# Down projection of a GeGLU feed-forward block: all 28 F blocks by Strassen, with a 20-block ring for the right operands

## The chip, the cores and the metric

The kernel runs on one core of one Trainium2 chip. The metric is the device time of one execution in microseconds; lower is better.

## The reference

```python
def setup_inputs():
    B, S, D, F = 1, 2048, 1024, 3584
    # x [B,S,D], w_gate [D,F], w_up [D,F], w_down [F,D]: bfloat16, normal * 0.05

def reference(x, w_gate, w_up, w_down):
    return (gelu_tanh(x @ w_gate) * (x @ w_up)) @ w_down
```

F is 28 blocks of 128. The kernel takes x in two halves of 1024 rows, and each half in two groups of 512 rows. For each half it makes the hidden tensor `hT` (gate, gelu, up, product), then two down groups.

## The kernel before

Nearly all matmuls are part of Strassen's scheme: a 2x2 product of blocks with seven block products M1 to M7 in place of eight. Sums of left operands are S1 to S4, of right operands T1 to T4. M1 and M2 read the bf16 tensors themselves; the other five read sums, or copies, held in fp32r (a 32-bit float type). B11 to B22 are the four quarters of a right operand, A11 to A22 those of a left one. A gate/up "pair" of F blocks takes 16 bf16 and 40 fp32r matmuls. A down group works on 11 block columns of each half of F by Strassen and on the 6 blocks left over by plain bf16 matmuls:

```python
NS = 11                                    # Strassen blocks in each half of K
NKK = (KF - 2 * NS) // WDT                 # 3 tiles of 2 plain blocks
t_mem = ...[P, max(5 * KH * TB, 2 * NS * DN)]   # right operands, two sets of 11
...
def down_group(hT, h, grp, then):          # then: work issued behind a product
    product("m1", PB, h_block(0, 0), wd_block(0, 0), True)
    product("m5", VB, lsum(0), rsum(0), True, behind=two(to_s2_t2))
    load_wd_to(base + 3)
    product("m2", PB, h_block(0, 1), wd_block(1, 0))
    product("m6", QB, lsum(0), rsum(0), behind=two(to_s4_t4), order=tail)
    product("m7", RB, lsum(1), rsum(1), behind=lambda i: t_down("b22", i, i + 1), order=head)
    ...                                    # additions; plain matmuls of bank set PB
    product("m3", QB, lsum(0), rsum(1), behind=two(next_s1_t3) if more else None)
    product("m4", RB, lsum(1), rsum(0), behind=two(next_t1) if more else None)
    ...                                    # the other plain matmuls, evacuation, stores
```

T2 and T4 of w_down are made once, while the pairs of the first half run ("staging": three subtractions for each block, the results stored to DRAM), and reloaded in each group by the SP queue (the queue in which SyncE issues transfers one after the other). In the first half the same queue also brings in the x of the second half, by transposing DMAs of one slice of 128 x 512 each, and the gate and up weights of its first pairs.

Two other places matter. In the startup, plain units (gate and up of one F block by bf16 matmuls, gelu, product) run while the operands of the first pair are made; in the passage to the second half, those of its first pair are made behind the down group:

```python
# startup                                  # passage, behind products of group 1
unit(hT, (0, 0), 0, 1)                     then1["m3"] = [lambda: w_fill(0)]
for name in S_NAMES:                       then1["m4"] = [t_sum t1, t2, t3]
    for j in range(2):                     then1["plain"] = [
        s_sum(0, PPG, j, name)  # GpSimd       t_sum b22, s_fill,  # s_fill: GpSimd
t_sum("t4")                     # GpSimd       t_sum t4,           # GpSimd
for fi in range(1, FPG):                       lambda: w_fill(1),
    unit(hT, (0, 0), fi, 1)                ]
```

## Time and profile before

| | before |
|---|---|
| time, median of 3 runs | 548.70 us (548.59 to 548.71) |
| span of the profiled run | 546.8 us |
| first matmul of the first down group | 187.13 us |
| first matmul of the second half | 277.07 us |
| first matmul of its first down group | 453.46 us |
| TensorE's gap at the end of the startup, from one matmul's start to the next | 0.36 us, from 36.45 us |

The page of the profile, the chain and the startup are shown and read in the prediction below.

### The profile page before, as it was taken

The page shows a single profiled execution, that of the slowest core. Times are in us where ns is not written, and L with a number is a line of the kernel's source. Part 1 is how long each engine was busy: PE and PEld are TensorE (multiplying, and loading weights), DVE is VectorE, ACT ScalarE, POOL GpSimd, SP SyncE. Part 2 cuts the span into 40 slices and gives each one's busy share as a digit, 9 for nine tenths or more (in the row PEclk, how much of TensorE's full clock was granted, in tenths as well). Part 3 has the DMA queues.
Part 4 walks back from the last instruction along what each step waited for, and adds up shares of the span by engine and source line. Part 5 has one row for each costly group of instructions (what it writes and reads, how often), then busy time and mean ns, then how long its engine had stood idle before and what let it go on. Part 6 is the DMA issues. An engine that isn't in the chain of part 4 may idle for free.

```text
span 546.8 us, 7160 instructions
## 1 busy us (share of the span) xinstructions
PE 538.7 (99%) x2390; PEld 364.9 (67%) x2433; DVE 305.4 (56%) x416; ACT 252.8 (46%) x446; POOL 253.4 (46%) x216
## 2 busy tenths in 40 slices
PE   8999999999999999999999999999999999999997
PEld 3456677777677667557667766777667776775673
DVE  1716666665566998934534444444444469986412
ACT  2435555555555317225365555555555542333161
POOL 0487767777666000000499776677776720000000
PEclk9999999999999999999999999999999999999999
DMA  9743364563725799579932240404040419904922
GB/s 271 229 133 122 98 226 142 166 196 113 230 79 192 254 345 292 144 264 319 331 130 78 76 130 24 155 1 154 0 155 5 150 61 316 352 4 161 354 102 77
DMA packets 69700, 90.65 MB, mean 166 GB/s; under 512 B 15904, under 2 KB 46624, under 8 KB 69664
## 3 DMA queue, kind: packets, MB, share of 16 engines
q1 hardware_dynamic: 69120, 89.67, 50.4%
q10 hardware_dynamic: 544, 0.52, 0.3%
q8 instruction: 20, 0.33, 0.2%
q14 instruction: 16, 0.13, 0.1%
HBM read 77.07 MB, written 9.96 MB: 159 GB/s over the span
## 4 chain that ended last, share of the span: by engine, by line
PE 97%; DMA 1%; issue 1%; ACT 0%; ACTq 0%
PE bank L368 60%; PE bank L569 33%; PE bank L232 5%; DMA w_mem<-in_w_up_dram 1%; PE bank L290 0%; ACT o_sb L721 0%; ACTq L155 0%
## 5 line engine op out<-in xcount | busy, mean ns | idle before, releaser
L368 PE MATMUL bank<-t_mem,s_mem 128*128 128x512 f32 x1040 | 255.2, 400 | 0.0
L368 PEld LDWEIGHTS bank<-t_mem,s_mem 128*128 128x128 f32 x1040 | 195.5, 188 | 45.2
L342 POOL TENSOR_TENSOR s_mem<-w_mem 128x512 fp32r<-128x512 bf16 x104 | 125.7, 1229 | 187.1 <-DMA w_mem<-in_w_gate_dram 112.0
L391 DVE TENSOR_TENSOR bank<-bank,m 128x512 f32<-128x512 f32 x104 | 72.4, 699 | 98.8 <-ACT bank L411 89.7
L251 DVE TENSOR_TENSOR hT<-w_mem,bank 128x512 bf16<-128x512 f32 x112 | 76.6, 687 | 63.9 <-ACT w_mem L246 31.1
L246 ACT ACTIVATE w_mem<-bank 128x512 f32<-128x512 f32 x112 | 66.4, 597 | 87.5 <-DVE bank L391 52.7
L569 PE MATMUL bank<-t_mem,s_mem 128*128 128x512 f32 x440 | 104.4, 395 | 0.0
L368 PE MATMUL bank<-xT,w_mem 128*128 128x512 bf16 x391 | 95.2, 380 | 1.5
L569 PEld LDWEIGHTS bank<-t_mem,s_mem 128*128 128x128 f32 x440 | 82.6, 188 | 18.4
L368 PEld LDWEIGHTS <-w_mem 128*128 128x128 bf16 x416 | 36.7, 98 | 50.5 <-issue 13.3
L569 PEld LDWEIGHTS <-hT 128*128 128x128 bf16 x368 | 34.9, 98 | 43.8 <-issue 3.7
L342 POOL TENSOR_TENSOR s_mem<-s_mem,w_mem 128x512 fp32r<-128x512 f32 x52 | 61.2, 1198 | 0.0
L342 POOL TENSOR_TENSOR s_mem<-w_mem,s_mem 128x512 fp32r<-128x512 bf16 x52 | 60.0, 1175 | 0.0
L499 DVE TENSOR_TENSOR t_mem<-w_mem 128x1024 fp32r<-128x1024 bf16 (+2 forms) x54 | 52.5, 1020 | 0.0
L355 ACT CAST s_mem<-w_mem 128x512 fp32r<-128x512 bf16 x52 | 31.9, 615 | 32.5 <-PE bank L368 29.1
L569 PE MATMUL bank<-wd_sb,hT 128*128 128x512 bf16 x184 | 41.4, 379 | 0.5
L569 PE MATMUL bank<-w_mem,hT 128*128 128x512 bf16 x169 | 39.0, 380 | 0.4
L406 ACT COPY m<-bank 128x512 f32<-128x512 f32 x52 | 30.5, 587 | 17.6 <-PE bank L368 17.6
L411 ACT COPY bank<-bank 128x512 f32<-128x512 f32 x52 | 29.6, 570 | 17.1 <-PE bank L368 17.1
L402 ACT COPY bank<-bank 128x512 f32<-128x512 f32 x52 | 29.6, 570 | 13.7 <-PE bank L368 13.7
L721 ACT CAST o_sb<-bank 128x512 bf16<-128x512 f32 x28 | 14.4, 620 | 43.9 <-PE bank L569 43.9
L548 DVE TENSOR_TENSOR s_mem<-hT 128x512 fp32r<-128x512 bf16 (+3 forms) x36 | 27.8, 804 | 6.6 <-PE bank L368 3.4
(31 smaller groups left out, 195.9 us busy)
## 6 DMA issues: line engine op xcount, KB each, us to landing
t_mem<-t_dram SPq DMA_DIRECT2D x32, 512.0 KB, 5.1
w_mem<-in_w_gate_dram SPq DMA_DIRECT2D x11, 1024.0 KB, 5.5
w_mem<-in_w_up_dram SPq DMA_DIRECT2D x11, 1024.0 KB, 7.9
w_mem<-in_w_down_dram SPq DMA_DIRECT2D x8, 1024.0 KB, 7.5
t_mem<-t_dram SPq DMA_DIRECT2D x24, 256.0 KB, 5.9
wd_sb<-in_w_down_dram SPq DMA_DIRECT2D x12, 512.0 KB, 5.7
wd_sb<-in_w_down_dram SPq DMA_DIRECT2D x22, 256.0 KB, 7.2
t_dram<-o_sb SPq DMA_DIRECT2D x22, 256.0 KB, 2.1
```

What stands on the lines that cost most here:

```text
L246: act(nc.scalar.activation(out=g_sb, in_=ps[:], func=ACT.Gelu_apprx_tanh))
L251: nc.vector.tensor_tensor(out=hT[:, fc, tb * TB : (tb + 1) * TB], in0=g_sb, in1=ps[:], op=ALU.mult,)
L342: pool(nc.gpsimd.tensor_tensor(out=t, in0=in0, in1=in1, op=op))
L355: act(nc.scalar.copy(out=t, in_=a(1, 1)))
L368: nc.tensor.matmul(banks[bank][:], lhsT=lhs[:, c, :], rhs=rhs[:, c, :], start=start and c == 0, stop=c == KH - 1, skip_group_check=True,)
L391: nc.vector.tensor_tensor(out=banks[dst][:], in0=banks[src][:], in1=m5[j][:], op=ALU.add)
L402: act(nc.scalar.copy(out=banks[QB[j]][:], in_=banks[PB[j]][:]))
L406: act(nc.scalar.copy(out=m5[j][:], in_=banks[VB[j]][:]))
L411: act(nc.scalar.copy(out=banks[RB[j]][:], in_=banks[QB[j]][:]))
L499: dve(nc.vector.tensor_tensor(out=t, in0=in0, in1=in1, op=ALU.subtract))
L548: dve(nc.vector.tensor_tensor(out=t, in0=in0, in1=in1, op=op))
L569: nc.tensor.matmul(banks[bank][:], lhsT=lhs, rhs=rhs, start=start, stop=stop, skip_group_check=True,)
```

## The change

The intent is to give the six plain blocks to Strassen too, which takes 196 matmuls for a group in place of 202. The operands of 14 blocks no longer fit in two fixed sets, so five right operands (T1, T2, T3, B22, T4) follow one another through a ring of 20 blocks, each new block in the place of one that has been read; B21 of w_down is streamed in as an operand of M2, and M2 moves behind M7. Staging covers 14 blocks, of which three move into the startup. T4 of gate/up, and the S sums of the second half's first pair, move from GpSimd to VectorE.

```diff
-    NS = 11
-    NKK = (KF - 2 * NS) // WDT
+    NS = KF // 2
+    NR = 20
-    t_mem = shared_pool.tile([P, max(5 * KH * TB, 2 * NS * DN)], F32R, name="t_mem")
+    t_mem = shared_pool.tile([P, NR * DN], F32R, name="t_mem")
@@ t_sum
             t2 = tsum["t2"].bitcast(F32)
-            pool(nc.gpsimd.tensor_tensor(out=t, in0=b(1, 0), in1=t2, op=sub))
+            dve(tt(out=t, in0=b(1, 0), in1=t2, op=sub))
@@ the ring
+    SEQ = ("t1", "t2", "t3", "b22", "t4")
+    def right(grp, name, i0, i1):
+        r0 = ((grp * len(SEQ) + SEQ.index(name)) * NS + i0) % NR
+        t = t_mem[:, r0 * DN : (r0 + i1 - i0) * DN]
@@ down_group, after M5 (B21 is loaded here, T2 to T4 behind the product before)
+        for q in range(4):
+            load_b21(n, q)
+        done("m5")
+        product("m6", QB, lsum(0), rsum("t2"), False, False, behind_m6, tail)
+        ...
+        def behind_m7(i):
+            if NT2 + i < NS:                       # NT2 = NR - NS = 6
+                t_down(grp, "b22", NT2 + i, NT2 + i + 2)
+            else:
+                t_down(grp, "t4", NT2 + i - NS, NT2 + i - NS + 2)
+        product("m7", RB, lsum(1), rsum("t3"), False, False, behind_m7, head)
+        ...
+        out22 = evacuate(VB, 1, 1)
+        done("m7")
+        store(out22)
+        product("m2", PB, h_block(0, 1), b21, False, True)
+        def behind_m3(i):
+            if NT2 + i < NS:
+                t_down(grp, "t4", NT2 + i, NT2 + i + 2)
+            ...
+        product("m3", QB, lsum(0), rsum("b22"), False, True, behind_m3)
+        ...
+        product("m4", RB, lsum(1), rsum("t4"), False, True, behind_m4, tail)
@@ startup
             t_sum("t4")
             for fi in range(1, FPG):
+                stage_sums(fi - 1)
+                stage_load(fi + 1)
                 unit(hT, (0, 0), fi, 1)
@@ behind the products of the first half's groups
-            for name in ("m7", "m3", "m4", "plain"):
-                then0[name] = then0.get(name, []) + x_fill(3)
-            then1["m6"] = x_fill(4)
-            then1["m3"] = [lambda: w_fill(0)]
+            then0["m5"] += x_fill(6)
+            then0["m6"] = x_fill(4)
+            then1["m5"] = x_fill(6)
+            then1["m6"] = [lambda: w_fill(0, 0)]   # gate weights
+            then1["m7"] = [lambda: w_fill(0, 1)]   # up weights
             ...                                    # t_sum and s_fill on VectorE, behind M3 and M4
```

## The prediction

> **What bounds the kernel now.** I read the page's busy times, its slices and its chain first, then the chain in order of time, then timelines of the two places where the change moves work between engines. All times are of the profiled run, 546.8 us long.
>
> ```profile
> PE 538.7 (99%) x2390; PEld 364.9 (67%) x2433; DVE 305.4 (56%) x416; ACT 252.8 (46%) x446; POOL 253.4 (46%) x216
> PE   8999999999999999999999999999999999999997
> POOL 0487767777666000000499776677776720000000
> PE 97%; DMA 1%; issue 1%; ACT 0%; ACTq 0%
> PE bank L368 60%; PE bank L569 33%; PE bank L232 5%; DMA w_mem<-in_w_up_dram 1%; PE bank L290 0%; ACT o_sb L721 0%; ACTq L155 0%
> ```
>
> TensorE sets the end nearly everywhere: 97% of the chain, and no slice between the first and the last below nine tenths. L368 are the gate/up pairs, L569 the down groups, L232 the plain first units. So a matmul less is time saved, and any new wait of TensorE is time lost, since nothing later has slack to take it up. GpSimd (POOL) is busy in slice 2 to 13, that is from 14 us, and idle in the down groups.
>
> ```profile
> 23.07 10.74 PE bank L232 x49
> 33.80 0.05 issue
> ...
> 48.98 12.55 PE bank L368 x55
> 61.52 0.05 issue
> ```
>
> This is the chain in order of time (start, length, what). Its pieces give the price of a matmul. Plain bf16: 10.74 + 0.05 us over some 50 of them, 0.2158 us each. One pair (16 bf16, 40 fp32r, 56 in all) is 12.60 us, so an fp32r matmul costs (12.60 - 16 x 0.2158)/40 = 0.229 us. The two down groups of the first half run from 187.13 to 277.07 us in the trace, 44.97 us each, with 92 bf16 and 110 fp32r matmuls by the code: (44.97 - 19.85)/110 = 0.2283 us. An fp32r matmul is thus 6% dearer than a bf16 one, and I use 0.2158 and 0.2283 below.
>
> Now the startup, where VectorE (DVE) and GpSimd work side by side, and the passage from the first half to the second:
>
> ```profile
> 22.96 2.65 DVE L223 TENSOR_TENSOR t_mem<-xT 128x2048 fp32r<-128x2048 bf16 x1
> 25.71 0.69 DVE L251 TENSOR_TENSOR hT<-w_mem,bank 128x512 bf16<-128x512 f32 x1
> 29.16 0.69 DVE L251 TENSOR_TENSOR hT<-w_mem,bank 128x512 bf16<-128x512 f32 x1 [2.76 <-PE bank L232]
> 32.62 0.69 DVE L251 TENSOR_TENSOR hT<-w_mem,bank 128x512 bf16<-128x512 f32 x1 [2.77 <-PE bank L232]
> 36.07 0.69 DVE L251 TENSOR_TENSOR hT<-w_mem,bank 128x512 bf16<-128x512 f32 x1 [2.77 <-PE bank L232]
> ```
> ```profile
> 23.94 2.68 POOL L342 TENSOR_TENSOR s_mem<-w_mem 128x512 fp32r<-128x512 bf16 x1 [0.48 <-DMA w_mem<-in_w_up_dram]
> 26.58 2.27 POOL L342 TENSOR_TENSOR s_mem<-s_mem,w_mem 128x512 fp32r<-128x512 f32 x2
> 28.80 2.27 POOL L342 TENSOR_TENSOR s_mem<-w_mem 128x512 fp32r<-128x512 bf16 x2
> 31.03 2.28 POOL L342 TENSOR_TENSOR s_mem<-w_mem,s_mem 128x512 fp32r<-128x512 bf16 x2
> 33.27 4.10 POOL L226 TENSOR_TENSOR t_mem<-xT,t_mem 128x2048 fp32r<-128x2048 bf16 x1
> ```
> ```profile
> 267.83 3.09 DVE L221 TENSOR_TENSOR t_mem<-xT,t_mem 128x2048 fp32r<-128x2048 bf16 x1
> 270.84 3.24 DVE L223 TENSOR_TENSOR t_mem<-xT 128x2048 fp32r<-128x2048 bf16 x1
> ```
>
> The reader is to see three things. From 25.6 to 36 us VectorE is idle but for one product per unit, while GpSimd runs its eight sums of the first pair back to back, about 1.1 us each. The last unit's product ends at 36.07 + 0.69 = 36.76 us, and TensorE's fifth matmul of the first pair, which writes the bank that this product reads, starts at 36.81 us: it already waits 0.15 us. So VectorE's last product in the startup has no slack at all. And the same 128x2048 operation takes 2.29 us where GpSimd is idle but 3.09 and 3.24 us where it is busy, while GpSimd's 128x512 sums stretch from 1.15 to 3.20 us.
>
> [...] 270.92 (end of the second operation) + one GpSimd sum of about 1.05 us + 2.2 us of own work = 274.1 us, the end of the third (270.84 + 3.24). [...] A product with one input in PSUM is not slowed (0.69 us beside busy GpSimd). [...] its warming matmuls stand 0.427 us apart, twice 0.2158.
>
> **The change part by part.**
> Matmuls. A group goes from 92 bf16 + 110 fp32r (11 Strassen blocks and 6 plain ones) to 56 bf16 + 140 fp32r (7 products x 14 blocks x 2 banks): 56 x 0.2158 + 140 x 0.2283 = 44.05 us against 44.97. That is 0.92 us less, 3.7 us over four groups. The six matmuls saved per group would be 1.3 us; the dearer kind takes back 0.4.
>
> VectorE in a group. Per 14 blocks: S sums 4 x 7 operations of 128x512 and T sums 2 x 7 of 128x1024, which start 0.605 and 1.14 us apart in the trace, and four additions of 0.61: 17 + 16 + 2.4 = 35.3 us of 44. It fits. The tight spot is product M7 of the first group: M5, M6 and M7 now follow one another without a bf16 product between. I walked it with those spacings, from the group's start at 0: M7 starts at 18.9, its T3 block 12 is needed at 24.4 and made by about 22.9. Slack 1.4 us, no stall. The ring's T2 and T4 reloads (512 KB each, near 0.4 MB per us in the packets) land 1 to 4 us early.
>
> Startup. T4 moves from GpSimd to VectorE, and the first three staging steps (three 128x512 subtractions each, two SBUF inputs) are put among the units. The built order on VectorE is: product, T4, three subtractions, product, three, product, three, product; the last product is the one without slack. GpSimd still has six sums to run from 26.6 us. Alternating: T4 from 26.6 to 28.8; six subtractions, each behind one GpSimd sum, 6 x (1.05 + 0.60) = 9.9, to 38.7; a product 0.6; three subtractions alone 3 x 0.72 = 2.2 (each needs the one before); last product 0.7: 42.2 us instead of 36.76. TensorE[...] stands from 36.7 to 42.2: +5.4 us.
>
> [...]
>
> Passage to the second half. The eight S sums of pair 0 and four T sums are now on VectorE: T1 can start 7.3 us before the group ends, and alone they end 6.3 us after it, in time for the addition that M3 of the pair waits for at 8.9 us. GpSimd's sums for the next pair start 2.7 us after the group's end and cost up to three alternations of 1.05 us: addition at about 10: +0.7 us, taken between 0 and 1.2.
>
> Sum: 548.7 - 3.7 + 5.4 + 1.0 + 0.7 = 552.1 us.
>
> **The rivals.** (a) The startup hides it: if GpSimd's sums didn't hold up 512-wide subtractions, T4 and six of them would end by 33.8 us and the last product at 37.5, +0.7 us; total about 545.7 us. For it: staging subtractions in the pairs show 0.68 to 0.69 us, never more. Against: there GpSimd happens to be idle; and at 51.44 us a GpSimd sum takes 1.30 us just where a subtraction ends. I give this 0.15. (b) VectorE or the reloads become the bound inside the groups: 35.3 of 44 us and 1 us of slack at the last block of a reload; queued transposes of x hold the SP queue 1.26 us each. A stall of 1 us in each of four groups would make 556 us. Chance 0.1. [...]
>
> **Range and chances.** Between the sum and rival (a) I choose 551.8 us, with 547.0 to 554.5 for 8 in 10: the main case with and without the clock and passage terms, and part of the way towards (a). Two per cent is 11 us. Faster by that would take three times the matmul saving (0.01); slower would need the startup stall and a stall in every group (0.02); within 2%: 0.97.
>
> **What would show it.** Down groups of 44.1 us each, and in the startup a GpSimd sum between each two subtractions, with TensorE's gap before the fifth matmul of the first pair ending at a VectorE product at about 42 us; matmuls about 0.43 us apart after the gap if the clock fell. I am wrong if that gap is under 2 us, if the groups take over 45 us, or if the clock term exceeds 2 us.

The sum came to 552.1 us: 548.7 us of before, -3.7 for the matmuls, +5.4 for the startup stall, +1.0 for the clock, +0.7 for the passage. The walk of the startup, a GpSimd sum of about 1.05 us ahead of each subtraction, is my estimate from the lines shown (two GpSimd sums in a row start 1.11 us apart in before, at 275.05 and 276.17 us).

## More of the kernel before

One view more is needed, the windows view over the two down groups of the first half. The columns are start and end of the window, its length, then busy microseconds (and instructions) of PE, PEld, DVE, ACT and POOL, then the granted TensorE clock, the DMA engines' busy share (the time of the packets that start in the window over that of 16 engines, so that it can pass 1) and GB/s.

```profile
187.13:276.90 89.77, 89.30 (x397) 58.81 (x405) 63.06 (x78) 33.74 (x63) 9.78 (x5) 1.00 0.91 281
```

TensorE is busy for 89.30 of 89.77 us, so nothing is waited for, but the last number but one says that the DMA engines are busy for 91% of that time.

## The result

| | before | after |
|---|---|---|
| time, median | 548.71 us (548.59 to 548.74, 4 runs) | 554.93 us (554.25 to 555.48, 4 runs) |
| span of the profiled run | 546.8 us | 553.1 us |
| startup gap of TensorE, start to start | 36.45 to 36.81 us | 36.57 to 41.58 us |
| down groups, first half | 44.97, 44.97 us | 46.22, 45.51 us |
| first to second half's down groups (14 pairs) | 176.39 us | 176.40 us |
| down groups, second half | 44.97 us each | 43.95 us each |

The outputs are correct. After is slower: the ratio is 1.0113, with a 95% interval of 1.0096 to 1.0131. A ratio here is the mean time of one kernel's fast runs over that of the other's of the same rounds, so not quite the ratio of the medians. The size is within 2%, as predicted, but 554.93 us lies 0.43 us above the top of the predicted range and 3.1 us above its centre.

Group times in the table are from the first matmul of M1 of one group to the first matmul of what follows, read off the instruction times in the trace. The page of after, with its busy times, slices, chain and two of its costliest groups:

```profile
PE 540.7 (98%) x2409; PEld 374.4 (68%) x2409; DVE 350.9 (63%) x465; ACT 259.8 (47%) x434; POOL 243.3 (44%) x206
PEclk9998999999999999999999999999999999999999
PE 87%; DMA 7%; DVE 4%; issue 1%; SPq 0%; ACT 0%; ACTq 0%; DVEq 0%
...
L600 PE MATMUL bank<-t_mem,s_mem 128*128 128x512 f32 x560 | 131.8, 393 | 2.1 <-DMA t_mem<-t_dram 2.1
...
L376 PE MATMUL bank<-xT,w_mem 128*128 128x512 bf16 x416 | 99.4, 382 | 4.6 <-DVE hT L255 4.6
```

TensorE's share of the chain fell from 97 to 87%. Two takers are named in the last two lines by what ended TensorE's idle time: 4.6 us ended by VectorE's product (`hT`) before the gate/up matmuls, and 2.1 us ended by a reload (`t_mem<-t_dram`) before down matmuls. A third, the fourth digit of PEclk, is a piece at a lower clock. (The waits for reloads measured below add up to more than the page's 2.1 us, which counts only the gaps ahead of single matmuls that it puts down to them.) The chain in order of time (start, length, what) gives the places:

```profile
28.89 1.57 DVE o_sb L548
...
40.84 0.69 DVE hT L255
...
41.58 152.14 PE bank L376 x668
...
228.63 9.32 DMA t_mem<-t_dram
...
275.07 8.41 DMA t_mem<-t_dram
...
285.45 176.40 PE bank L376 x784
...
461.85 87.91 PE bank L600 x392
```

From 285.45 us to the end of the last group the chain is TensorE alone: the fourteen pairs 176.40 us, that is 14 x 12.60, and both groups of the second half 87.91 us. So after loses nothing in the second half. It loses in the startup, where the chain runs through VectorE's staging subtractions (L548), and once in each group of the first half, where it runs through a reload.

Startup, timelines of VectorE and GpSimd (start, length, instruction; x2 means two):

```profile
28.82 1.64 DVE L548 TENSOR_TENSOR o_sb<-wd_sb 128x512 fp32r<-128x512 bf16 x1
30.49 3.09 DVE L548 TENSOR_TENSOR o_sb<-wd_sb,o_sb 128x512 fp32r<-128x512 bf16 x2
...
39.51 1.42 DVE L548 TENSOR_TENSOR o_sb<-wd_sb,o_sb 128x512 fp32r<-128x512 bf16 x2
```
```profile
31.43 3.16 POOL L350 TENSOR_TENSOR s_mem<-w_mem 128x512 fp32r<-128x512 bf16 x2
34.55 3.18 POOL L350 TENSOR_TENSOR s_mem<-w_mem,s_mem 128x512 fp32r<-128x512 bf16 x2
```

The staging subtractions are L548. Two take 3.09 us while GpSimd has sums left and 1.42 us when it has none; a GpSimd sum takes 1.59 us (3.18/2), not 1.14. The last product ends at 41.53 us, against 42.2 predicted.

Then the first half's reloads. The windows view of after (columns as above):

```profile
41.58:45.50 3.92, 3.92 (x11) 2.76 (x11) 0.00 (x0) 1.16 (x2) 0.66 (x1) 0.56 0.94 308
193.70:237.90 44.20, 43.13 (x190) 29.94 (x187) 40.70 (x51) 16.67 (x26) 0.00 (x0) 1.00 0.93 272
238.08:283.60 45.52, 44.66 (x196) 31.34 (x197) 31.57 (x40) 19.09 (x30) 0.00 (x0) 1.00 0.92 294
461.85:505.80 43.95, 43.95 (x197) 31.62 (x196) 40.45 (x51) 17.25 (x27) 0.00 (x0) 1.00 0.70 226
```

The first window is the half clock after the stall, 0.56 on average; in finer windows it is 0.50 from 42.01 to 45.42 us, for 3.41 us, and 1.00 before and after. The others are two groups of the first half and one of the second: nearly the same instructions, VectorE no busier in one than in the other, the clock full in all; the DMA engines are at 92 to 93% in the first half and at 70% in the second, where there is no next x and no next weight to bring. The waits lie at the last blocks of M4, for which the timeline of TensorE in group 0 has three stretches such as this one:

```profile
238.08 1.17 PE L600 MATMUL bank<-t_mem,s_mem 128*128 128x512 f32 x4 [0.53 <-DMA t_mem<-t_dram]
```

And the SP queue's timeline of that group shows why the reload came late:

```profile
206.50 17.34 SPq L172 DMA_TRANSPOSE xT<-in_x_dram  x10
223.95 1.46 SPq L520 DMA_DIRECT2D t_mem<-t_dram  x3
...
226.66 2.29 SPq L520 DMA_DIRECT2D t_mem<-t_dram  x4
```
```profile
218.70:223.95 5.25, 5.25 (x26) 2.42 (x26) 4.57 (x8) 5.25 (x11) 0.00 (x0) 1.00 0.44 100
```

The first three reloads of T4 fill ring blocks that M7 had freed by 218.7 us; they are issued at 223.95 us, behind ten transposes that hold the queue for 17.34 us. The second view is the windows view of the 5.25 us between: the DMA engines are busy for only 44% of them, at 100 GB/s. So at this point it is the order and hold of the queue that keeps the reloads back, and not full engines, whatever the average of 93% says. Then seven reloads and two stores of outputs go out within 5 us, and the last, issued at 228.63, lands 9.32 us later at 237.95; M4 needed it at about 236. In group 1 the transposes are over by 264.2 us and the reloads are issued on time, but between two megabytes of weights; the last one takes 8.41 us to land.

**The account.** Matmuls: four groups of 43.95 in place of 44.97, -4.1 us. Startup stall: the waiting matmul starts at 41.58 us in place of 36.81, +4.77 us. Half clock: from the first matmul after the stall to the first down group 151.98 us, against 150.32 before: +1.66. Reload waits: 46.22 - 43.95 and 45.51 - 43.95: +3.84. Passage: none. Sum +6.2 us; the two spans differ by 553.1 - 546.8 = 6.3.

### The profile page after: what moved, and what is told of

Its sections match the earlier page's. It is cut to its first block, busy times and chain, and to the rows that moved or that the text cites. A ratio compares the mean times of both kernels' runs of the same rounds, so it can differ in the third digit from the quotient of the medians.

```text
span 553.1 us, 7231 instructions
## 1 busy us (share of the span) xinstructions
PE 540.7 (98%) x2409; PEld 374.4 (68%) x2409; DVE 350.9 (63%) x465; ACT 259.8 (47%) x434; POOL 243.3 (44%) x206
## 4 chain that ended last, share of the span: by engine, by line
PE 87%; DMA 7%; DVE 4%; issue 1%; SPq 0%; ACT 0%; ACTq 0%; DVEq 0%
PE bank L376 59%; PE bank L600 25%; DMA t_mem<-t_dram 5%; PE bank L232 3%; DMA w_mem<-in_w_up_dram 1%; DVE o_sb L548 1%; DVE s_mem L575 1%; DVE t_mem L525 1%; DMA wd_sb<-in_w_down_dram 1%; DVE t_mem L226 0%; DVE hT L255 0%; SPq L520 0%; PE bank L294 0%; DVE bank L634 0%; ACT o_sb L648 0%
## 5 line engine op out<-in xcount | busy, mean ns | idle before, releaser
L376 PE MATMUL bank<-t_mem,s_mem 128*128 128x512 f32 x1040 | 256.6, 401 | 0.0
L376 PEld LDWEIGHTS bank<-t_mem,s_mem 128*128 128x128 f32 x1040 | 196.5, 189 | 45.8 <-issue 0.3
L350 POOL TENSOR_TENSOR s_mem<-w_mem 128x512 fp32r<-128x512 bf16 x100 | 122.8, 1247 | 205.5 <-PE bank L376 185.7
L600 PE MATMUL bank<-t_mem,s_mem 128*128 128x512 f32 x560 | 131.8, 393 | 2.1 <-DMA t_mem<-t_dram 2.1
L600 PEld LDWEIGHTS bank<-t_mem,s_mem 128*128 128x128 f32 x560 | 104.6, 188 | 27.1 <-issue 4.5
L376 PE MATMUL bank<-xT,w_mem 128*128 128x512 bf16 x416 | 99.4, 382 | 4.6 <-DVE hT L255 4.6
L255 DVE TENSOR_TENSOR hT<-w_mem,bank 128x512 bf16<-128x512 f32 x104 | 71.3, 687 | 50.5 <-ACT w_mem L250 26.3
L250 ACT ACTIVATE w_mem<-bank 128x512 f32<-128x512 f32 x104 | 61.8, 596 | 79.4 <-DVE bank L399 46.1
L525 DVE TENSOR_TENSOR t_mem<-w_mem 128x1024 fp32r<-128x1024 bf16 x56 | 65.6, 1219 | 0.0
L575 DVE TENSOR_TENSOR s_mem<-hT 128x512 fp32r<-128x512 bf16 x56 | 36.6, 686 | 9.1 <-PE bank L600 7.0
L600 PEld LDWEIGHTS <-hT 128*128 128x128 bf16 x224 | 21.3, 98 | 26.6 <-issue 2.1
L232 PE MATMUL bank<-xT,w_mem 128*128 128x512 bf16 x128 | 28.1, 379 | 0.3 <-DMA w_mem<-in_w_up_dram 0.2
L522 ACT CAST t_mem<-w_mem 128x1024 fp32r<-128x1024 bf16 x28 | 26.9, 1047 | 0.0
```

The lines of the kernel that those rows point to most:

```text
L232: return nc.tensor.matmul(ps[:], lhsT=w_sb[:, kd, fi * P : (fi + 1) * P], rhs=xT[:, kd, tb * TB : (tb + 1) * TB], start=(kd == 0), stop=(k ...
L250: act(nc.scalar.activation(out=g_sb, in_=ps[:], func=ACT.Gelu_apprx_tanh))
L255: nc.vector.tensor_tensor(out=hT[:, fc, tb * TB : (tb + 1) * TB], in0=g_sb, in1=ps[:], op=ALU.mult,)
L350: pool(nc.gpsimd.tensor_tensor(out=t, in0=in0, in1=in1, op=op))
L376: nc.tensor.matmul(banks[bank][:], lhsT=lhs[:, c, :], rhs=rhs[:, c, :], start=start and c == 0, stop=c == KH - 1, skip_group_check=True,)
L525: dve(nc.vector.tensor_tensor(out=t, in0=in0, in1=in1, op=ALU.subtract))
```

## The experiments

The theory after the result: three separate costs. (1) VectorE's staging subtractions in the startup are slowed by GpSimd's sums beside them, and so delay the last product. (2) The idle time that follows halves the clock, and this costs 1.66 us by itself. (3) The reloads of T4 are late in the first half because other transfers stand ahead of them. Rivals: for (1), the subtractions are slow by themselves or are waiting for staging data; for (2), the lost 1.66 us is another wait; for (3), the ring itself is too small, or VectorE too busy, so that the waits would be there without other transfers. All ratios below are to before in the same rounds; after stands at 1.0113.

**The clock alone: 20 dummy matmuls inside the stall (e1).**

```diff
         for j in range(2):
+            if h == 0 and pair == PPG and j == 1:
+                for _ in range(20):                    # writes a bank that M5 starts anew
+                    pe(nc.tensor.matmul(banks[VB[0]][:], lhsT=warm_l, rhs=warm_r,
+                                        start=True, stop=True, skip_group_check=True))
             mm(PB[j], j, block(key, j, 0, 0), b11, True)
```

Theory A is (2).

> Twenty dummy bf16 matmuls into a free bank stand in the stall of the startup, before the fifth matmul of the first pair; 20 x 0.216 = 4.3 us, less than the stall of 4.8. Theory A [...]: the trace shows full clock throughout, the pair goes on at the same time, 41.6 us, and the kernel takes 553.2 to 553.4 us. Rival C (the slow matmuls after the stall come from something else, a cold queue or the DMA): the time stays at 554.9.

Correct; 553.76 us (553.15 to 554.84), ratio 1.008 (1.006 to 1.010). The windows view of the time of the stall and of the time after it:

```profile
36.70:42.50 5.80, 5.80 (x28) 2.60 (x27) 5.62 (x8) 0.57 (x1) 1.23 (x1) 1.00 0.88 247
42.50:46.50 4.00, 4.00 (x19) 3.06 (x18) 0.00 (x0) 1.86 (x4) 1.96 (x2) 1.00 1.02 347
```

The clock stays at 1.00 where it had been 0.56, and TensorE does 19 matmuls in 4 us, against 11 in 3.9. In this profile the startup ran later, with the fifth matmul at 42.51 us and not at 41.6 as expected; but from there to the first down group it is 150.33 us, against 151.98 in after and 150.32 before. That shows (2). The ratio fell by 0.0033, 1.8 us, against 1.66 us in the account; its interval overlaps after's, so the time alone would not have shown it. The stall itself stayed, as it should.

**Staging out of the startup (e2).** The three staging steps are done two at a time in the pairs that follow.

```diff
             for fi in range(1, FPG):
-                stage_sums(fi - 1)
-                stage_load(fi + 1)
                 unit(hT, (0, 0), fi, 1)
@@ in the first three pairs: stage_load of 2p+2 and 2p+3, and behind M4
-                    then["m4"] = [lambda i=i: stage_sums(i)]
+                    then["m4"] = [sums(2p), load(2p+3), sums(2p+1)]
```

> The three staging steps leave the startup and go to the first three pairs, two steps a pair. Theory A: the startup's last product ends near 36.8 us again, no stall, no clock drop: -4.9 - 1.7 = 6.5 us less, 548.4 us; still -4.1 for the matmuls and +3.8 for the late reloads against before. Rival (VectorE has too much to do in those pairs, the wait only moves): 552 to 554 us, with TensorE waiting for an addition of VectorE in pairs 2 to 4.

Correct; 548.86 us (548.56 to 549.23), ratio 0.9989 (0.9974 to 1.0004). TensorE's gap is 0.36 us again, at 36.5 us, and the clock is 1.00 throughout. That is 0.0124 of ratio, 6.8 us, for the stall and the half clock, which the account has at 4.77 + 1.66 = 6.4 us. With T4 still on VectorE, the last product ends at 36.82 us: it is the staging, and not T4's move, that made the stall. The reload waits stayed (groups of 46.08 and 45.25 us), so they don't come from the stall.

**GpSimd's first sums without reads (e3).** Wrong on purpose (relative error 0.288): GpSimd's eight sums of the first pair are replaced by fills with zero, which read nothing. They wait for no weights either, and so run at once: from 0.87 to 4.99 us, long before the subtractions, beside which GpSimd does nothing at all in this run.

```diff
+            elif h == 0 and pair == PPG:
+                pool(nc.gpsimd.memset(t.bitcast(F32), 0.0))
             else:
                 pool(nc.gpsimd.tensor_tensor(out=t, in0=in0, in1=in1, op=op))
```

Theory A is (1).

> GpSimd's eight sums of the first pair become fills with zero, which read no SBUF; the result is wrong on purpose. VectorE's order is unchanged. Theory A [...]: subtractions 0.69 us each, the last product ends by 38 us, TensorE waits about 1 us instead of 4.8, the clock stays up: 549 to 549.8 us. Rival B (the queue on VectorE is too long whatever GpSimd does): subtractions stay at 1.0 to 1.6 us and the time at 554.9.

549.53 us (549.07 to 551.06), ratio 1.0006 (0.9985 to 1.0027). The same place in VectorE's timeline, the first staging subtractions, and the last product:

```profile
28.41 0.68 DVE L550 TENSOR_TENSOR o_sb<-wd_sb 128x512 fp32r<-128x512 bf16 x1
29.13 1.42 DVE L550 TENSOR_TENSOR o_sb<-wd_sb,o_sb 128x512 fp32r<-128x512 bf16 x2
...
36.19 0.68 DVE L255 TENSOR_TENSOR hT<-w_mem,bank 128x512 bf16<-128x512 f32 x1
```

A subtraction takes 0.68 us in place of 1.64, and two 1.42 in place of 3.09. The last product begins at 36.19 us in place of 40.84, and TensorE's gap is 0.59 us (the third staging step waits 0.34 us for its load). VectorE's program and the staging loads are the same, and only GpSimd's work beside them is gone: (1) is shown, and the rival that the subtractions or their data are slow by themselves has fallen. That it is GpSimd's reads, and not any work of GpSimd, this run does not separate, since no fill ran beside a subtraction.

**Four transposes behind the reloads (group 0) (e4).**

```diff
-            then0["m6"] = x_fill(4)
+            then0["m3"] = x_fill(4)
```

> Only the place of four transposing loads of x in the first group changes: from after M6 to after M3, behind the reloads of T4. The bytes are the same. Theory A (T4's first reloads wait behind transposes in the one in-order queue): the first group falls from 46.2 to about 44 us, the kernel to 552.7 us. Rival D (it is the bytes, the DMA engines are full): the group stays at 46 us or the wait moves to M6 of the second group, 554 to 555 us.

Correct; 553.27 us (552.57 to 554.15), ratio 1.0068 (1.0046 to 1.009). The SP queue's timeline:

```profile
215.25 4.83 SPq L172 DMA_TRANSPOSE xT<-in_x_dram  x3
220.19 1.46 SPq L520 DMA_DIRECT2D t_mem<-t_dram  x3
```

The reloads are issued at 220.19 us, at the end of the remaining six transposes, and group 0 takes 43.94 us: no wait is left, with the ring, VectorE's work and all transfers of the group the same. (In the other runs with the old order, e1, e2, e3 and e6, this wait is 1.1 to 2.1 us: its size varies, but none is without it.) Group 1, untouched, keeps its wait (45.46 us). So in group 0 it is the place of four transposes in the queue that makes the wait, and the ring is large enough. The edit also puts half a megabyte less ahead of the reloads; that the queue and not these bytes held them is what the 44% in the view above says. The ratio fell by 0.0045, 2.5 us, for the 2.27 us of the wait. In this run the half clock lasted about 6.8 us (the granted clock is 0.77 in 37 to 42 us and 0.62 in 42 to 48), against 3.41 in after, and cost about 2.1 us.

**The 16 transposes as 4 of four slices each (e5).** The same bytes in all, two behind M5 of either group: eight slices in each, in place of ten and six.

```diff
-            slices = [(tb, kd) for tb in range(NTB) for kd in range(KD)]
+            slices = [(tb, kd) for tb in range(NTB) for kd in range(0, KD, 4)]
-                    fs.append(lambda tb=tb, kd=kd: load_xT(xT, nh, tb, kd, kd + 1))
+                    fs.append(lambda tb=tb, kd=kd: load_xT(xT, nh, tb, kd, kd + 4))
-            then0["m5"] += x_fill(6)
-            then0["m6"] = x_fill(4)
-            then1["m5"] = x_fill(6)
+            then0["m5"] += x_fill(2)
+            then1["m5"] = x_fill(2)
```

> The 16 transposing loads of x, one slice each, become four of four slices each, eight slices per group; all else as in the changed kernel, startup stall included. Theory A (one-slice transposes hold the in-order queue 1.26 us each and move only 0.1 MB per us): the queue is free for T4 earlier in both groups, both first-half groups fall to about 44 us, the kernel to 551.1 us. Rival D (the bytes are what is late): the groups stay at 46.2 and 45.5 us, 554 to 555 us.

Correct; 553.37 us (552.57 to 554.18), ratio 1.0073 (1.0055 to 1.0092). Groups 43.95 and 44.42 us, so the waits fell from 3.84 to 0.47 us. Group 1's fell too, from 1.57 us, although two slices more and the same weights stand ahead of its reloads. But the total fell by 2.2 us only (0.0040 of ratio), because two other terms grew in this run: the half clock again lasted about 6.8 us (0.86 granted in 36 to 42 us and 0.61 in 42 to 48.5; about 2.4 us lost in place of 1.66), and a wait of 1.3 us came up in the second half's first pair. This is the passage wait that the prediction had: the reload wait had hidden it, since it kept TensorE back while VectorE worked on.

**Fewer bytes ahead of group 1's reloads (e6).** The up weights of the second half's first pairs (1 MB) are loaded behind M3 in place of M7.

```diff
-            then1["m7"] = [lambda: w_fill(0, 1)]
             then1["m3"] = [
+                lambda: w_fill(0, 1),
                 lambda: t_sum("t1"),
```

> In the second group the 1 MB of up weights for the next half is asked for after M3 instead of after M7, so behind all of T4's reloads. If the bytes ahead of T4 make the second group's wait (rival D for that group), that group loses its 1.6 us wait in M4, while the sums of the up weights come late and M5 of the next pair waits up to 3 us: in all 553.5 to 556 us. If it is the transposes alone, the group's wait stays at 1.6 us.

Correct; 563.07 us (562.39 to 563.18), ratio 1.0252 (1.0237 to 1.0268): slower, and by far more than I had expected. Group 1 does lose its wait (44.25 us in place of 45.51), which shows that the weights ahead of the reloads made it, though not alone: with transposes by four (e5, e7, e9) it is 0.42 to 0.47 us with the weights in their place. But the second half's pairs take 185.7 us in place of 176.4. VectorE's timeline (the bracket is the idle time ahead and what ended it) and TensorE's:

```profile
286.55 0.69 DVE L348 TENSOR_TENSOR s_mem<-w_mem 128x512 fp32r<-128x512 bf16 x1 [6.34 <-DMA w_mem<-in_w_up_dram]
```
```profile
291.17 3.56 PE L376 MATMUL bank<-t_mem,s_mem 128*128 128x512 f32 x8 [2.67 <-DVE t_mem L221]
```

VectorE stands 6.34 us at an S sum of up for the late weights, and everything behind it, T2 and T4 of the pair above all, is late by as much. TensorE waits twice, 2.67 and 2.10 us in its timeline, and its matmuls are slower behind each of the two waits: eight from 291.17 us take 3.56 us, where the eight from 296.12 take 2.20, and five from 300.43 us take 1.87, where five take 1.43 in e7 (from 285.79). The mean granted clock of the run is 0.990, against 0.997 in after. I had counted one wait of the length of the weights' delay, and had missed both that all of VectorE's work behind it is held up and that the matmuls slow down twice.

**Both causes out: staging late and transposes by four (e7).** The edits of the second and the fifth experiment together.

> Staging out of the startup (as in e2) and the transposes by four (as in e5). Theory A: no startup stall, no clock drop, no reload wait: the four groups at 43.95 us, -4.1 us against before, 544.6 us where before takes 548.7. Rival: the reload waits remain, 548.4 us.

Correct; 546.76 us (545.59 to 547.17), ratio 0.9954 (0.9936 to 0.9972): a gain, but 2.2 us short of the 544.6 expected. Groups 44.27 and 44.37 us, 0.7 us of waits, clock 1.00 throughout. The passage wait is there, 1.26 us, ended by a VectorE addition; VectorE's timeline ahead of it:

```profile
278.74 3.23 DVE L348 TENSOR_TENSOR s_mem<-w_mem,s_mem 128x512 fp32r<-128x512 bf16 x2
281.89 3.24 DVE L226 TENSOR_TENSOR t_mem<-xT,t_mem 128x2048 fp32r<-128x2048 bf16 x1
```

The two S4 sums take 3.23 us where they take 1.29 with GpSimd idle, and T4 3.24 in place of 2.29: GpSimd's sums for the next pair have begun at 278.59 us.

**Both causes out, the other way: staging late and the four transposes behind M3 (e8).**

> Staging out of the startup (as in e2) and the four transposes after M3 (as in e4). Theory A: first group 43.95 us, second group still 45.5: 546.2 us where before takes 548.7. Rival: the wait of the first group moves to the second, 548.4 us.

Correct; 547.12 us (545.87 to 548.02), ratio 0.9963 (0.9942 to 0.9983), 0.9 us above what was expected. Groups 43.95 and 45.82 us, pairs of the second half 176.41 us: group 1's wait is left, and with it no passage wait. Together with e7 this fits the view that either the one or the other shows.

**GpSimd later in the passage (e9).** The edits of staging late and transposes by four, and in the second half's first pair GpSimd's S1 and S2 for the next pair are issued behind M7. Theory A is that the passage wait comes from these sums running beside VectorE's S4 and T4 (3.23 and 3.24 us in e7).

```diff
-            prep(j, "s1")                  # behind M5; likewise "s2" behind M6
+            if not first_of_half:
+                prep(j, "s1")
...
+        if first_of_half:                  # behind M7
+            for name in ("s1", "s2"):
+                for j in range(2):
+                    prep(j, name)
```

> As the run with both repairs (staging out of the startup, transposes by four); besides, in the first pair of the second half GpSimd's sums for the next pair stand behind M7 in its queue instead of behind M5. Theory A [...]: the 1.3 us wait goes, VectorE's T4 takes 2.29 us instead of 3.24; 1.2 us less than before the edit, ratio to before near 0.993. Rival (VectorE's queue is too long there by itself): the wait stays, ratio 0.995 to 0.996.

Correct; 546.58 us (545.55 to 547.19, 6 runs), ratio 0.9953 (0.9938 to 0.9967). The passage wait is gone: T4 takes 2.28 us, GpSimd starts at 283.94 us, and the pairs take 176.40 us. That shows the cause of the passage wait, but over e7 the time did not move measurably (0.9954 and 0.9953), and the expected 0.993 was missed. In this profile group 1 has 0.44 us of reload wait, as it had in e7 (0.42), and the second half's first group a wait of 0.34 us, where e7 had none; such tenths vary from run to run.

**Two stores later (e10).** The same with the first two stores of a group behind M3, so that fewer bytes stand ahead of the reloads of T4.

```diff
         out22 = evacuate(VB, 1, 1)
         done("m7")
-        store(out22)
...
-        store(out11 + evacuate(QB, 0, 1))
+        store(out22 + out11)
+        store(evacuate(QB, 0, 1))
```

> As e9; besides, the two stores of the first finished quarter are issued after M3 instead of after M7, so behind all of T4's reloads. If the rest of the reload waits (0.3 to 0.4 us in each first-half group) is bytes ahead of T4 in the queues, 0.25 MB less means 0.6 us earlier and both waits go: 0.5 to 0.7 us less than e9. If ScalarE's evacuations then wait for buffers, TensorE waits at the next group and the time is e9's or worse.

Correct; 545.92 us (545.10 to 547.68, 6 runs), ratio 0.9943 (0.9927 to 0.9958). Groups 43.97, 44.15 and, in the second half, 43.95 us: the reload waits are gone but for 0.2 us in group 1. In return ScalarE's evacuations wait for a store to free their buffer, and the second half's first pair for ScalarE, 0.6 us in the profile (pairs 177.03 us). This is the best version, 0.6% faster than before and, by the two ratios, 1.7% faster than after (0.9943/1.0113), but its interval overlaps that of e9, so the last step by itself is inconclusive.

## Why the prediction was wrong

The direction and the main mechanism were right; the number was 3.1 us too low, and the range missed by 0.43 us. By its own steps:

| step | predicted | measured | |
|---|---|---|---|
| matmuls, four groups | -3.7 | -4.1 | right; 43.95 us a group, not 44.05 |
| startup stall | +5.4 | +4.77 | right in mechanism (e2, and e3 without GpSimd's sums) and nearly in size |
| half clock | +1.0 | +1.66 | right that the idle time halves the clock (0.50 in after, 1.00 in e1) |
| reloads of T2 and T4 | 0 | +3.84 | wrong: the step that failed |
| passage | +0.7 | 0 | hidden behind the reload waits |
| sum | +3.4 | +6.2 | |

**The step that failed** is "The ring's T2 and T4 reloads (512 KB each, near 0.4 MB per us in the packets) land 1 to 4 us early". For T2 no wait shows. T4's last blocks came late enough to cost 2.27 us in group 0 and 1.57 in group 1. The step reckoned each reload with the queue and the engines to itself. What it left out is in two views of before that I had at hand: the transposes' hold on the SP queue, 1.26 us each, which the prediction names only under rival (b), and the DMA engines' 91% in the first half's groups. In group 0 the hold came first: the blocks were free at 218.7 us, the reloads issued at 223.95, with the engines at 44% between; only then did seven reloads fill the engines (84 to 103% in the profile), and the last took 9.32 us. Two transposes of four slices hold the queue for 11.60 us in this place (e7; 12.07 in e10), against 17.34 for the ten of one slice. The change puts 7 MB of reloads into a group in place of 5.5 (14 of 512 KB; before, 8 of 512 and 6 of 256), and it places ten transposes directly ahead of T4's. Moving four of these away took the whole wait of group 0 (e4); moving 1 MB of weights took 1.26 of the 1.57 us of group 1's (e6), and transposes by four took 1.10 (e5). Groups of over 45 us are one of the prediction's own signs of being wrong. Rival (b) had this stall, at 0.1 and in all four groups; it came only in the two of the first half, where x and weights share the queue.

**The stall was sized well** because it was worked out by single instructions, and in part by luck: the walk with a GpSimd sum ahead of each subtraction gave 42.2 us, the trace 41.53, and two errors offset each other. The walk had left out one product, 0.6 us, and had given each of six subtractions 1.65 us; five took 1.52 to 1.64, and the one behind a product 1.04: the GpSimd sum beside it had begun at 32.99 us, ahead of the product, and was over at 34.59. Rival (a), that GpSimd wouldn't hold up 512-wide subtractions, fell: the first one took 1.64 us, and 0.68 with GpSimd idle. But the walk is not good everywhere: in the passage of after, T4 started at 288.39 us, 0.2 us behind a GpSimd sum, and took its undisturbed 2.29 us, while that sum took 3.50 us and the next 1.15.

**The clock** was granted at 0.50 for 3.41 us in after, which cost 1.66 us; the 1.0 us was a mean over a fall and none. TensorE was idle for 4.63 us in the stall of after, and for 2.98 us of the 3.41 ahead of the drop (38.60 to 42.01 us; TensorE's ends are modelled). In all four profiled runs that kept the stall empty the clock fell (mean granted clock 0.997 in after, 0.994 in e4 and e5, 0.990 in e6); with the stall filled (e1) or gone (e2, e3, e7) the mean is 1.000. In e4 and e5 the half clock lasted about 6.8 us and cost 2.1 to 2.4 us, so 1.66 us was not the upper end.

**Small slips.** GpSimd is not idle to the end of the down groups: in the prediction's own line of slices it is busy again in slice 20, before 277 us. And of GpSimd's eight sums in the startup two are over at 26.6 us, so that six and its T4 run beside the idle VectorE. None of these moved the sum.

**The passage** of 0.7 us was the right mechanism: 1.26 us of it appear when the reload wait is taken away, and none when GpSimd begins later. In after it cost nothing, since the two waits do not add up: while TensorE waits for group 1's reload, VectorE gets ahead.

**The gain** was real. Four groups of 43.95 us are worth 4.1 us, and e10 keeps about 3 of them. It was lost to a stall, 3.41 us at half clock and a held DMA queue, and not in the matmuls.

## What to carry to other kernels

When a change adds transfers to a stage, list what its queue holds ahead of them, in issue order with the time that each holds the queue, and read the DMA share of that stage, piece by piece: an average of 93% hid 5 us at 44%. T4's last four reloads in group 0 landed in 7.3 to 9.3 us, not in the kernel's median of 5.8, and "free early enough" does not mean "issued early enough". A cheap two-input operation put in front of the last VectorE product on the path cost here as much as the GpSimd sums beside it (1.52 to 1.64 us for a 128x512 subtraction, 1.60 for a sum, where they take 0.68 and 1.15 alone), so side work belongs in a stage where both engines have slack. And waits on one path hide each other: taking 3.4 us of reload waits away brought up 1.3 us in the passage (e5), so price a fix by running it.
